# A hand-tuned order of work, shifted: a range flag and its register loads get earlier due times, and a new table of due-time offsets replaces the old one

## The chip, the cores and the metric

The kernel runs as one program on one core of a Trainium2 chip. The metric is device time in microseconds (us), the median of several executions. Five engines work side by side, each through its own queue of instructions in program order: TensorE (PE, with its weight loads listed as PEld), VectorE (DVE), ScalarE (ACT), GpSimd (POOL) and SyncE (SP). SP does little but issue DMA transfers; its issues are listed under SPq.

## The reference

The computation is a gated linear-attention scan followed by a two-layer MLP whose activation is a smooth gate.

```python
def _attn_ref(q, k, v, a_re, a_im):        # 4 batches, 8 heads, 768 steps, 48 wide
    mag = np.sqrt(a_re * a_re + a_im * a_im)
    scale = np.minimum(mag, 0.999) / (mag + 1e-06)
    a_re_n, a_im_n = (a_re * scale, a_im * scale)
...
    for t in range(S):
        ar, ai = (a_re_n[:, :, t, :, None], a_im_n[:, :, t, :, None])
        new_re = ar * S_re - ai * S_im
        new_im = ar * S_im + ai * S_re
        kv = np.einsum('bhd,bhe->bhde', k[:, :, t], v[:, :, t])
        S_re, S_im = (new_re + kv, new_im)
        y[:, :, t] = np.einsum('bhd,bhde->bhe', q[:, :, t], S_re)

def _moe_ref(x, w_in, w_out):              # x 3072x384, w_in 384x2048, w_out 2048x384
    h = x @ w_in
    g = np.where(h >= 1, h, np.where(h <= -1, 0.0, (h + 1) ** 2 / 4.0))
    return (g @ w_out).astype(np.float32)
```

## The kernel before

**Tiling.** The 3072 tokens are cut into 12 units u of 256 tokens (u0 to u11), and two units make one of 6 blocks (512 tokens). A unit goes through these steps:

- `gates(u)`: DVE and ACT turn the decays into running products (tiles ai_u) and multiply them into queries and keys. Its two last DVE operations, here called the *turns*, are one line, L984: one writes x_u, the other kq_u, each 128x1536.
- `spread`: ten DMAs on SP's queue (helper line L554) carry x_u and kq_u into the head layout hd_u_0, hd_u_1, hd_u_2. Of each of the two sources there are two pieces of 288 KB (48x1536), one of 128 KB (32x1024) and two of 32 KB (16x512).
- `attend(u)` on PE, in four short visits: *scores* (L1138, 32 small matmuls on hd_u, into banks that DVE masks at L1150), transposes (L1078), products (L1107) and values (L1182, L1190). The result goes by xr DMAs into the layout of the MLP.
- `split(blk)`: ACT writes xH (L1285), DVE the remainder xL (L1292).
- `moe(blk)`: the first product h (L1319), the gate (ACT s L1345, DVE g L1364 and L1372, ACT gh L1378, DVE gl L1382) and the second product o (L1396), in 16 steps f per block. A matmul of L1319 or L1396 is called a *MoE matmul* below; there are 1746 of 512 columns or their equal.

**Beside that.** `weights` decodes the packed weights early on: a load raw_i or raw_o (768 KB, L569), then on DVE y (L584), two merges (L593, L602) and the low part wi or wo (L613). `ranges` loads the packed weights a second time late in the run (tiles chk, L569) and sums them in two ACT passes each (L660, L668). From these sums and those of the gates nine tiny DVE operations (L1508 to L1516) make the *flag*; one PE matmul (L1519) and two DVE operations (L1520, L1524) finish it; five register loads (L1532 on ACT, POOL, DVE and SP, L1543 on PE) and a branch (L1547) read it. The branch leads to a general path that these inputs don't take. The last three results are copied out of PSUM at L1434 (ob) and stored by L554.

**What sets the order.** All operations are recorded first, with `pl.op`, and class `Plan` then writes the queues. `order` gives each operation a due time: the given `due=`, or the least of its successors' due times less its own duration, plus an offset from the table NUDGE under the operation's number, if it has one. Offsets thus pass on to all that an operation needs. Then a list scheduler takes, engine by engine, what is ready and due first; for DVE, ACT and SP it may hold a place for something that is due sooner. BEGIN[NBLK] is the due time at the end of the last block, the numbers are in ns. `emit` writes the result, and until the first MoE matmul `warm` adds idle matmuls (L1459) where PE would stand still. A waiting instruction blocks what is behind it on its engine, whatever that is.

## Time and profile before

| what | us |
|---|---|
| median of 3 executions (least, most) | 564.18 (564.12, 564.68) |
| the profiled execution's own time | 563.74 |
| its span, from first to last record | 561.9 |
| PE busy in the span | 548.6 |
| DVE busy | 438.8 |
| ACT busy | 395.3 |
| granted TensorE clock over the span | 1.00 |

The profiled execution is 0.44 us below the median, and 1.8 us of its time lie outside the span. Idle time of an engine is given with the instruction before which it fell, and with what released that instruction ("<-DMA hd<-kq" is the landing of a DMA that wrote hd from kq).

### The profile page before, as it was taken

The page shows a single profiled execution, that of the slowest core. Times are in us where ns is not written, and L with a number is a line of the kernel's source. Part 1 is how long each engine was busy: PE and PEld are TensorE (multiplying, and loading weights), DVE is VectorE, ACT ScalarE, POOL GpSimd, SP SyncE. Part 2 cuts the span into 40 slices and gives each one's busy share as a digit, 9 for nine tenths or more (in the row PEclk, how much of TensorE's full clock was granted, in tenths as well). Part 3 has the DMA queues.
Part 4 walks back from the last instruction along what each step waited for, and adds up shares of the span by engine and source line. Part 5 has one row for each costly group of instructions (what it writes and reads, how often), then busy time and mean ns, then how long its engine had stood idle before and what let it go on. Part 6 is the DMA issues. An engine that isn't in the chain of part 4 may idle for free.

```text
span 561.9 us, 10693 instructions
## 1 busy us (share of the span) xinstructions
PE 548.6 (98%) x4246; PEld 459.5 (82%) x4246; DVE 438.8 (78%) x611; ACT 395.3 (70%) x638; POOL 4.1 (1%) x27
## 2 busy tenths in 40 slices
PE   8999999989999999999999999999999999999997
PEld 8878777878888888888888888888888888888885
DVE  5999999989979888887996948898885743554643
ACT  6987987978977667766656663867556642469973
POOL 2000000000000000000000000000000000000000
PEclk9999999999999999999999999999999999999999
DMA  8587475463731604416200552606255300087631
GB/s 351 238 251 250 132 270 196 125 236 117 227 107 43 190 37 117 157 58 175 101 2 3 159 170 64 211 2 180 94 169 162 114 1 1 27 315 253 255 110 63
DMA packets 23686, 80.56 MB, mean 143 GB/s; under 512 B 4560, under 2 KB 10320, under 8 KB 23632
## 3 DMA queue, kind: packets, MB, share of 16 engines
q1 hardware_dynamic: 23488, 79.71, 42.4%
q8 instruction: 34, 0.56, 0.4%
q14 instruction: 20, 0.16, 0.1%
q10 hardware_dynamic: 144, 0.13, 0.1%
HBM read 55.05 MB, written 4.72 MB: 106 GB/s over the span
## 4 chain that ended last, share of the span: by engine, by line
PE 85%; DVE 10%; ACT 1%; issue 1%; DMA 1%; SPq 1%; POOL 0%; DVEq 0%; POOLq 0%; ACTq 0%
PE o L1396 33%; PE h L1319 32%; PE at L1138 5%; PE at L1182 3%; PE at L1190 3%; PE at L1107 2%; PE idle L1459 2%; PE at L1078 2%; DMA hd<-kq 1%; DVE x L984 1%; DVE kq L984 1%; PE o L821 1%; DVE g L1364 1%; SPq L554 1%; DVE gl L1382 1%
## 5 line engine op out<-in xcount | busy, mean ns | idle before, releaser
L1396 PE MATMUL o<-gh,wo 128*128 128x512 f32 x576 | 180.3, 394 | 0.0
L1319 PE MATMUL h<-xH,wi 128*128 128x512 f32 (+1 forms) x582 | 179.3, 390 | 0.9 <-ACT wo L637 0.6
L1319 PEld LDWEIGHTS h<-xH,wi 128*128 128x128 f32 x582 | 106.5, 188 | 23.7 <-DVE g L1364 1.1
L1396 PEld LDWEIGHTS o<-gh,wo 128*128 128x128 f32 x576 | 106.3, 188 | 22.4 <-issue 0.3
L1319 PE MATMUL h<-xL,wi 128*128 128x512 f32 (+1 forms) x291 | 112.4, 386 | 0.4 <-DVE xL L1292 0.4
L1396 PE MATMUL o<-gl,wo 128*128 128x512 f32 x288 | 112.3, 390 | 0.0
L1364 DVE TENSOR_TENSOR g<-h,s 128x512 f32<-128x512 f32 x95 | 65.3, 687 | 52.1 <-ACT s L1345 50.1
L1345 ACT ACTIVATE s<-h,cst 128x512 f32<-128x512 f32 x95 | 64.3, 685 | 44.9 <-PE h L1319 36.6
L1378 ACT CAST gh<-g 128x512 fp32r<-128x512 f32 x96 | 59.0, 617 | 33.9 <-DVE g L1372 24.7
L1382 DVE TENSOR_TENSOR gl<-g,gh 128x512 fp32r<-128x512 f32 x96 | 65.4, 685 | 14.6 <-ACT gh L1378 13.4
L1319 PEld LDWEIGHTS h<-xL,wi 128*128 128x128 f32 x291 | 54.6, 188 | 12.1 <-DVE xL L1292 0.8
L1396 PEld LDWEIGHTS o<-gl,wo 128*128 128x128 f32 x288 | 54.0, 188 | 11.5
L1372 DVE SCALAR_TENSOR_TENSOR g<-s,g 128x512 f32<-128x512 f32 x80 | 55.2, 691 | 2.2
L764 ACT ACTIVATE ai<-ai 128x768 f32<-128x768 f32 x48 | 40.3, 845 | 9.5 <-DVE ai L927 5.3
L1150 DVE COPY_PREDICATED am<-tri,at 128x512 f32<-128x512 uint32 x44 | 32.2, 740 | 7.6 <-PE at L1138 7.1
L1138 PE MATMUL at<-hd 96*64 96x64 f32 (+1 forms) x704 | 34.3, 249 | 3.1 <-DMA hd<-kq 3.1
L1138 PEld LDWEIGHTS at<-hd 96*64 96x64 f32 x704 | 31.6, 137 | 6.6 <-issue 4.2
L847 DVE TENSOR_TENSOR_SCAN ai<-again,ai 128x768 f32<-128x768 uint8 x20 | 35.0, 1749 | 0.4 <-ACT ai L764 0.2
L1190 PE MATMUL at<-am,V 128*64 128x128 f32 x352 | 32.9, 273 | 0.0
L1182 PE MATMUL at<-hd,st 96*64 96x128 f32 x304 | 30.5, 278 | 0.4 <-DVE am L1150 0.4
L564 ACT ACT_TABLE_LOAD x23 | 29.5, 1283 | 0.4
L764 ACT ACTIVATE x<-ai 128x768 f32<-128x768 f32 x27 | 22.3, 842 | 9.2 <-DVE ai L847 9.1
(133 smaller groups left out, 640.5 us busy)
## 6 DMA issues: line engine op xcount, KB each, us to landing
chk<-in_wl_dram SPq DMA_DIRECT2D x16, 768.0 KB, 4.6
kq<-in_kq_dram SPq DMA_DIRECT2D x12, 768.0 KB, 6.3
ai<-in_ari_dram SPq DMA_DIRECT2D x10, 768.0 KB, 6.2
V<-in_v_dram SPq DMA_DIRECT2D x12, 576.0 KB, 5.0
hd<-x SPq DMA_DIRECT2D x24, 288.0 KB, 3.4
hd<-kq SPq DMA_DIRECT2D x24, 288.0 KB, 4.2
raw_i<-in_wl_dram SPq DMA_DIRECT2D x8, 768.0 KB, 7.0
raw_o<-in_wl_dram SPq DMA_DIRECT2D x8, 768.0 KB, 5.0
```

Source lines behind the costliest of these rows:

```text
L764: lambda: A_.activation(out(), src(), f, **kw),
L847: lambda: V_.tensor_tensor_scan(dst().rearrange("p j t -> p (j t)"), again, src().rearrange("p j t -> p (j t)"), 0.0, op0=ALU.mult, op1=AL ...
L1138: PE_.matmul(SC.get()[o : o + HC, i + e, HC * k :], t[:, 0, ks], t[:, 1, qs], start=True, stop=True,)
L1182: PE_.matmul(o_, st.get().rearrange("p h e -> p (h e)")[:, lo : lo + 64], head(h)[:, 1, cs], start=True, stop=False,)
L1190: PE_.matmul(o_, V.get()[:, c, lo : lo + 64], ams[pr // 2].get()[:, 2 * (pr % 2) + e, :], start=st is None, stop=True,)
L1319: PE_.matmul(H.get()[:, lo:hi], weight["i", f // 2].get()[:, f % 2, part, sl], x.get()[:, j, lo:hi], start=j == 0 and n == 0, stop=j == NJ ...
L1345: lambda: A_.activation(SS.get(), H.get(), AF.Relu, bias=c_half, scale=-0.5 if spare else 0.5),
L1364: lambda: V_.tensor_tensor(G.get(), H.get(), SS.get(), op=ALU.max),
L1372: lambda: V_.scalar_tensor_tensor(G.get(), SS.get(), 1.0, G.get(), op0=ALU.min, op1=ALU.mult),
L1378: pl.op("ACT", act(T), lambda: A_.copy(GH.get(), G.get()), r=[G], w=[GH])
L1382: lambda: V_.tensor_tensor(GL.get(), G.get(), GH.get().bitcast(F32), op=ALU.subtract),
L1396: PE_.matmul(PO[m].get(), weight["o", f // 2].get()[:, f % 2, part, sl], g.get(), start=f == 0 and n == 0, stop=f == NF - 1 and n == 2,)
```

## The change

Three edits. The table NUDGE, some 650 offsets, is replaced by one of some 1200; a constant SOON = 6000 (ns) is added; and the nine flag operations of DVE and the four register loads of ACT, POOL, DVE and SP are due SOON ahead of the end of the plan. Nothing that is computed changes; instructions only take other places in their queues. The lines of the kernel move down by 35 (by 36 behind the new constant): L984 becomes L1020, L554 becomes L590, and so on.

```diff
 NUDGE = {
-    27: -14199.79, 28: -34500, 43: 134562.2, 53: -303446.36, 57: -4700, 58: -19660, 59: -78000,
...
+    23: 177054, 24: -34026, 25: 653, 29: -110195, 38: 300, 40: 12000, 53: -168116, 54: -375702,
...
 STAY = 300
+SOON = 6000
...
-        pl.op("DVE", 150, fn, w=[OK], after=marks, due=BEGIN[NBLK])
+        pl.op("DVE", 150, fn, w=[OK], after=marks, due=BEGIN[NBLK] - SOON)
...
                 lambda reg=reg: nc.reg_load(reg, ok[0:1, 0:1]),
                 r=[OK],
                 after=[gated[-1]],
-                due=BEGIN[NBLK],
+                due=BEGIN[NBLK] - SOON,
```

Where the table moves things is seen in the queues. The first place is SP's queue around the spread of u3. In the rows below hd_3_0 to hd_3_2 are the three head tiles, 48x1536 are pieces of 288 KB, 32x1024 of 128 KB and 16x512 of 32 KB; loads have a name that ends in _dram on the right. Before:

```order
L554 DMA hd_3_0_1144<-x_3_732 48x1536
L554 DMA hd_3_1_1151<-x_3_732 48x1536
L554 DMA hd_3_2_1158<-x_3_732 32x1024
L554 DMA hd_3_2_1158<-x_3_732 16x512 x2
L554 DMA hd_3_2_1158<-kq_3_854 16x512 x2
L554 DMA hd_3_2_1158<-kq_3_854 32x1024
L554 DMA hd_3_1_1151<-kq_3_854 48x1536
L554 DMA hd_3_0_1144<-kq_3_854 48x1536
L554 DMA kq_4_1210<-in_kq_dram 128x1536
L569 DMA raw_o5_1241<-in_wl_dram 128x1536
L554 DMA ai_5_1248<-in_ari_dram 128x1536
```

And now, in the changed kernel:

```order
L590 DMA hd_3_2_1144<-x_3_731 32x1024
L590 DMA hd_3_2_1144<-x_3_731 16x512
L590 DMA hd_3_1_1153<-x_3_731 48x1536
L590 DMA hd_3_2_1144<-x_3_731 16x512
L590 DMA hd_3_0_1165<-kq_3_831 48x1536
L590 DMA hd_3_1_1153<-kq_3_831 48x1536
L590 DMA hd_3_2_1144<-kq_3_831 32x1024
L590 DMA hd_3_2_1144<-kq_3_831 16x512 x2
L590 DMA hd_3_0_1165<-x_3_731 48x1536
L590 DMA ai_5_1222<-in_ari_dram 128x1536
L590 DMA kq_4_1236<-in_kq_dram 128x1536
L605 DMA raw_o5_1309<-in_wl_dram 128x1536
```

The last piece of the spread is now one of x_3, and the first loads behind it, ai_5 and kq_4, go into buffers that x_3 and kq_3 held, so their instructions wait on SP until the spread has read those out.

The second place is DVE between the two turns of u4 (its turns are the rows with x_4 and kq_4 on the left). Before:

```order
L984 TENSOR_TENSOR x_4_1170<-kq_4_1210,ai_4_849 128x1536
L1364 TENSOR_TENSOR g_0_12_1528<-h_0_12_1401,s_0_12_1477 128x512
L602 SCALAR_TENSOR_TENSOR raw_o6_1405<-raw_o6_1405 128x768
L1364 TENSOR_TENSOR g_0_13_1547<-h_0_13_1422,s_0_13_1519 128x512
L1382 TENSOR_TENSOR gl_0_12_1555<-g_0_12_1528,gh_0_12_1539 128x512
L984 TENSOR_TENSOR kq_4_1210<-kq_4_1210,ai_4_849 128x1536
```

Now:

```order
L1020 TENSOR_TENSOR x_4_1167<-kq_4_1236,ai_4_843 128x1536
L620 TENSOR_SCALAR y_o6_1500<-raw_o6_1446 128x768
L629 SCALAR_TENSOR_TENSOR raw_o6_1446<-raw_o6_1446,y_o6_1500 128x768
L1400 TENSOR_TENSOR g_0_13_1513<-h_0_13_1368,s_0_13_1481 128x512
L638 SCALAR_TENSOR_TENSOR raw_o6_1446<-raw_o6_1446 128x768
L620 TENSOR_SCALAR y_o7_1549<-raw_o7_1453 128x768
L1418 TENSOR_TENSOR gl_0_13_1553<-g_0_13_1513,gh_0_13_1529 128x512
L629 SCALAR_TENSOR_TENSOR raw_o7_1453<-raw_o7_1453,y_o7_1549 128x768
L649 TENSOR_TENSOR wo_6_1555<-raw_o6_1446,wo_6_1555 128x2x384
L638 SCALAR_TENSOR_TENSOR raw_o7_1453<-raw_o7_1453 128x768
L1400 TENSOR_TENSOR g_0_14_1584<-h_0_14_1455,s_0_14_1547 128x512
L1020 TENSOR_TENSOR kq_4_1236<-kq_4_1236,ai_4_843 128x1536
```

Counted from the start of the queue, six operations that stood behind the kq_4 turn stand ahead of it now (y_o7, both merges of raw_o7, wo_6, one g and one gl), and none has gone the other way.

The third place is PE near its end (at0_109<-ok4_121 is the flag's matmul, ok_123 the register's word). Before:

```order
L1396 MATMUL o2_114<-gh_5_15_5306,wo_7_1618 128x512 x2
L1396 MATMUL o2_114<-gl_5_15_5314,wo_7_1618 128x512
L1519 MATMUL at0_109<-ok4_121,cst_86 1x4
L1543 TENSOR_LOAD ok_123
```

Now:

```order
L1432 MATMUL o1_113<-gl_5_12_5270,wo_6_1555 128x512
L1432 MATMUL o2_114<-gh_5_12_5245,wo_6_1555 128x512 x2
L1432 MATMUL o2_114<-gl_5_12_5270,wo_6_1555 128x512
L1555 MATMUL at0_109<-ok4_121,cst_86 1x4
L1432 MATMUL o0_112<-gh_5_11_5232,wo_5_1402 128x512 x2
L1432 MATMUL o0_112<-gl_5_11_5239,wo_5_1402 128x512
```

The flag's matmul stood behind the last MoE matmul and now stands ahead of the last 33; PE's own register load keeps its place behind all of them.

Counted in the same way, these moved too. Of the MoE matmuls of the whole run, so many stand ahead of the first scores of a unit, before and now: u2 63 and 63, u3 183 and 180, u4 288 and 315, u5 441 and 423. Ahead of the kq turn DVE has, against before, one merge of raw_i3 (L602) less and one L1119 more at u2, one merge of raw_o4 (L593) less at u3, the six more at u4, and four less at u5 (a g pair, one xL, one gl). Behind the kq turn of u4 SP now issues eight transfers instead of six, with a 288 KB piece sixth and a 128 KB piece last; behind that of u5 it still issues seven, with a 288 KB piece sixth. On ACT four range passes that stood behind gh of the last block's step 11 stand ahead of it, and PE's first matmul that reads that tile has 60 MoE matmuls from itself to the end instead of 54. The stretches of attention that interrupt the MoE matmuls were 49 and are 46, the flag's matmul among them.

## Rows read from the trace of the kernel before

**Rows 1.** The page's first part: busy time of each engine, share of the span, and instructions.

```profile
PE 548.6 (98%) x4246; PEld 459.5 (82%) x4246; DVE 438.8 (78%) x611; ACT 395.3 (70%) x638; POOL 4.1 (1%) x27
```

**Rows 2.** Busy time by stretch of the span. Columns: stretch and its length, then PE, PEld, DVE, ACT and POOL busy with their counts, then granted clock, DMA share, GB/s.

```profile
59.00:120.00 61.00, 56.10 (x445) 45.68 (x444) 58.59 (x79) 54.20 (x82) 0.00 (x0) 1.00 0.62 208
...
160.00:540.00 380.00, 380.00 (x2778) 317.86 (x2774) 279.23 (x385) 247.06 (x411) 0.00 (x0) 1.00 0.36 116
500.00:542.00 42.00, 42.00 (x187) 34.77 (x186) 20.27 (x31) 38.09 (x77) 0.00 (x0) 1.00 0.65 236
```

**Rows 3.** Timeline of PE, the rows with idle time ahead of them at the scores of u2, at values of u2 and at the scores of u3. Columns: start, duration, engine, line, operation, tiles, shape, count, and in brackets the idle time before and its releaser.

```profile
73.88 1.63 PE L1138 MATMUL at<-hd 96*64 96x128 f32 x32 [1.14 <-DMA hd<-kq]
86.95 0.44 PE L1182 MATMUL at<-hd,st 96*64 96x128 f32 x4 [0.39 <-DVE am L1150]
...
115.51 1.56 PE L1138 MATMUL at<-hd 96*64 96x128 f32 x32 [1.96 <-DMA hd<-kq]
```

**Rows 4.** The chain of waits in the window 100 to 120 us, its piece ahead of the scores of u3: start, duration, what. (A DMA's time counts from its issue to its landing.)

```profile
110.11 5.27 DMA hd<-kq
```

**Rows 5.** Timeline of SP's queue at the spread of u3, with the load behind it.

```profile
103.02 3.24 SPq L554 DMA_DIRECT2D hd<-x  x5
106.36 4.33 SPq L554 DMA_DIRECT2D hd<-kq  x5
110.81 0.53 SPq L554 DMA_DIRECT2D kq<-in_kq_dram  x1
```

**Rows 6.** The same at the end of the spread of u2, with the load behind it.

```profile
70.52 0.52 SPq L554 DMA_DIRECT2D hd<-kq  x1
73.00 0.35 SPq L569 DMA_DIRECT2D raw_i<-in_wl_dram  x1
```

**Rows 7.** The DMA view of that last issue of u2: tiles, engine, count, KB each, median us from issue to landing.

```profile
hd<-kq SPq DMA_DIRECT2D x1, 288.0 KB, 3.3
```

**Rows 8.** DVE's groups by line, over the whole run: busy us and mean ns of one, then the idle time before them.

```profile
L1382 DVE TENSOR_TENSOR gl<-g,gh 128x512 fp32r<-128x512 f32 x96 | 65.4, 685 | 14.6 <-ACT gh L1378 13.4 <-PE o L1396 0.7
L1364 DVE TENSOR_TENSOR g<-h,s 128x512 f32<-128x512 f32 x95 | 65.3, 687 | 52.1 <-ACT s L1345 50.1 <-ACT s L1359 0.2
...
L593 DVE SCALAR_TENSOR_TENSOR raw_o<-raw_o,y_o 128x768 uint32<-128x768 uint32 x8 | 7.6, 955 | 0.1
...
L613 DVE TENSOR_TENSOR wo<-raw_o,wo 128x768 fp32r<-128x768 f32 x6 | 5.7, 948 | 0.0
...
L584 DVE TENSOR_SCALAR y_o<-raw_o 128x768 uint32<-128x768 uint32 x8 | 4.4, 552 | 0.0
```

**Rows 9.** Timeline of DVE: its wait at the first mask of u3; the kq turn of u4 and the row behind it; an xL, and the row behind the kq turn of u5.

```profile
116.45 0.73 DVE L1150 COPY_PREDICATED am<-tri,at 128x512 f32<-128x512 uint32 x1 [2.04 <-PE at L1138]
...
143.41 1.75 DVE L984 TENSOR_TENSOR kq<-kq,ai 128x1536 f32<-128x1536 f32 x1
145.08 0.95 DVE L613 TENSOR_TENSOR wo<-raw_o,wo 128x768 fp32r<-128x768 f32 x1
...
180.59 0.95 DVE L1292 TENSOR_TENSOR xL<-xr,xH 128x768 fp32r<-128x768 f32 x1
...
185.52 0.68 DVE L1364 TENSOR_TENSOR g<-h,s 128x512 f32<-128x512 f32 x1
```

**Rows 10.** Timeline of PE at the scores of u4 and of u5.

```profile
150.18 1.63 PE L1138 MATMUL at<-hd 96*64 96x128 f32 x32
...
193.88 1.56 PE L1138 MATMUL at<-hd 96*64 96x128 f32 x32
```

**Rows 11.** Timeline of SP's queue at the kq pieces of u4 and at the last issues of u5.

```profile
145.19 3.05 SPq L554 DMA_DIRECT2D hd<-kq  x5
...
190.36 1.41 SPq L554 DMA_DIRECT2D hd<-kq  x2
```

**Rows 12.** Timeline of all engines at the end: the last MoE matmul, the flag's matmul, the last store, the last flag operation.

```profile
557.28 0.39 PE L1396 MATMUL o<-gl,wo 128*128 128x512 f32 x1
...
557.60 0.19 PE L1519 MATMUL at<-ok,cst 128*1 128x4 f32 x2
...
558.57 0.34 SPq L554 DMA_DIRECT2D out_dram<-ob  x1
558.63 0.14 DVE L1524 TENSOR_SCALAR ok<-ft 1x1 int32<-1x1 f32 x1
```

**Rows 13.** The DMA view of that last store: KB each, median us from issue to landing.

```profile
out_dram<-ob SPq DMA_DIRECT2D x1, 128.0 KB, 1.7
```

**Rows 14.** Timeline of PE around one visit of attention late in the run, among MoE matmuls.

```profile
469.73 0.39 PE L1319 MATMUL h<-xL,wi 128*128 128x512 f32 x1
...
471.09 0.39 PE L1396 MATMUL o<-gl,wo 128*128 128x512 f32 x1
471.41 1.56 PE L1138 MATMUL at<-hd 96*64 96x128 f32 x32
...
473.46 0.39 PE L1319 MATMUL h<-xL,wi 128*128 128x512 f32 x1
```

**Rows 15.** Timeline of ACT at gh of step 11 of the last block, with a range pass behind it, and of PE at its first use of that tile.

```profile
541.52 0.62 ACT L1378 CAST gh<-g 128x512 fp32r<-128x512 f32 x1 [1.48 <-DVE g L1372]
542.05 0.91 ACT L660 ACTIVATE chk<-chk 128x768 f32<-128x768 f32 x1
...
545.27 0.61 PE L1396 MATMUL o<-gh,wo 128*128 128x512 f32 x2
```

243 rows, old and new, of the table NUDGE are left out of this document.

## The prediction

> **What bounds the kernel now.** I read the page's busy times first, then busy time by stretch, then PE's timeline for the rows that have idle time ahead of them, and last, from each of those, the chain of waits and the queues behind it. PE is busy 548.6 of a span of 561.9 us [rows 1], and from 160 to 540 us it is busy 380.00 of 380.00 [rows 2]. In that stretch a reordering can only win by fewer interruptions of the MoE matmuls. What it can win lies in 59 to 120 us, where PE is busy 56.10 of 61.00 and DVE 58.59 [rows 2]: DVE is nearly full there, and PE waits for what DVE makes. PE's three waits that hang on attention are 1.14 us at the scores of u2, 0.39 at values of u2 and 1.96 at the scores of u3, 3.49 in sum [rows 3]. The sum below is made on the profiled execution (span 561.9, own time 563.74), whose offset of 0.44 to the median is taken as fixed, so differences are applied to 564.18.
>
> **The wait at u3, and why it holds all that is ahead of it.** The scores of u3 start at 115.51, when the last piece of the spread has landed [rows 3]. That piece was issued at 110.11 and took 5.27 us [rows 4]; the load of kq_4 was issued behind it at 110.81, 0.70 us later [rows 5]. At u2 a last piece of the same 288 KB, issued at 70.52, took 3.3 us, and the next load came only at 73.00, 2.48 us later [rows 6, 7]. I take from this pair that a load on the heels of a spread delays its last piece by up to 5.27 - 3.3 = 1.97 us. In the changed kernel the two loads behind the spread of u3 need the buffers that the spread reads, so none can be issued before the pieces have been read out, and the last piece is again one of 288 KB: 3.3 us is the value nearest to it, 5.27 the other bound.
>
> The turns come earlier as well: one merge of raw_o4 (0.955 us, of which some 0.08 overlaps with its neighbour, as the 1.75 us turn at 143.41 whose follower starts 1.67 later shows) no longer stands ahead of them [rows 8, 9], which is 0.87. SP's issues run on without a gap from 103.02 to 110.69 [rows 5], so the last issue moves by the same 0.87, to 109.24, and the landing to 112.54. With 0.14 from landing to first matmul, as before, the scores start at 112.68 instead of 115.51: 2.83 earlier. But three fewer MoE matmuls stand ahead of them. One starts 0.227 us after the other ((471.09 - 469.73) / 6) [rows 14], so 0.68 of work is only put off. Net: **-2.15**.
>
> PE can be there in time: without its wait it was ready at 113.55, less 0.68 is 112.87, and the waits of u2, up to 1.53 [rows 3], shrink too (the turn is about 0.4 earlier and its last pieces are small ones). If they didn't, PE's 112.87 would set the start instead of 112.68. For the same reason what the table changes ahead of that point, in the head too, counts nothing of its own: PE waits at u3 anyway, and DVE's set of work there is the same but for the merge. Bounds: with a landing of 5.27 the gain is 0.87 - 0.68 = 0.19; it can't exceed the three waits, 3.49.
>
> **What the Trainium skill would make of it.** The row shows 5.27 us with a load 0.70 behind and 3.3 without [rows 4 to 7]. The Trainium skill, "DMA: Bandwidth & Descriptors", section "Queues, rings and completion order", says that each DMA engine consumes the descriptors of one ring in order. By that rule a load issued behind the pieces on the same queue can't hold them up, keeping it away gains nothing, and the sum would have -0.19 in place of -2.15. The pair of rows speaks against it, but it is one pair, in different surroundings; so it is a rival.
>
> **New waits at u4.** DVE gets six more operations ahead of the kq_4 turn: y_o7 0.55, two merges of 0.955, wo_6 0.95, g 0.69, gl 0.69, less 0.08 each: 4.3 us [rows 8]. Against that, DVE's own wait of 2.04 us for the scores of u3 [rows 9] goes with the scores 2.83 earlier. So the turn starts at 143.41 - 2.04 + 4.3 = 145.67 and ends 1.67 later, at 147.34. Eight issues follow at 0.61 each (3.05 for five) [rows 11]; the sixth, of 288 KB, starts at 150.5 and lands at 153.8 (3.3) to 155.8 (5.27), the last, of 128 KB, starts at 151.7 and lands at 155.0, for head tile 2, which the last of the 32 scores read. PE is there at 150.18 - 2.83 + 6.81 (30 more MoE matmuls between the scores of u3 and these) = 154.2 [rows 10]. Wait: 0 to 1.6; **+0.2**, since 153.8 is in time and the small one nearly.
>
> **New waits at u5.** DVE has 2.7 us less ahead of the kq_5 turn (an xL of 0.95, a g pair at 0.69 each, a gl of 0.69, less overlaps) [rows 8, 9]. That turn ended at 185.52, and now ends at 180.8 if the 2.04 is kept, else at 182.8. Before, the last issue ended at 191.77 [rows 11], seven issues in 6.25. The sixth, of 288 KB, starts after five, so at 184.0 (0.61 each) to 185.4 (0.89 each), and lands at 187.3 to 188.7, or up to 190.7 without the 2.04. PE is there at 193.88 - 2.83 + 0.2 - 3.4 (15 fewer MoE matmuls since the scores of u3) = 187.9 [rows 10]. Wait: 0 to 2.8; **+0.4**.
>
> **The flag.** Its matmul leaves the very end and interrupts PE 33 MoE matmuls ahead of it. Its own two passes took 0.19 [rows 12]; an interruption of 32 scores took 473.46 - 471.09 - 3 x 0.227 = 1.69 for rows of 1.56, 0.13 more [rows 14]; at the most the 0.32 from the last start at 557.28 to 557.60 [rows 12] and that 0.13 again. **+0.35** (0.2 to 0.45). Its gain at the end: the flag was done at 558.77, but the last store, issued at 558.57, lands 1.7 later, at 560.3 [rows 12, 13], so loads and branch have 1.5 us of cover. That store still waits for the last MoE matmul and two copies. **0** (0 to -0.1 while the cover holds; without it at most the 0.2 from 558.57 to 558.77). If the DVE operations of the flag stood badly they would block gl; they are nine of under 0.2 us on an engine with 20.27 busy of 42 [rows 2].
>
> **Interruptions.** 46 instead of 49, the flag's among the 46, so four of attention are gone at 0.13 or a little less: **-0.3** (0 to -0.5). Later units come after fewer MoE matmuls than before; DVE is busy 279.23 of 380 there [rows 2], which is their cover; 0 (up to +0.5 without it).
>
> **Sum:** -2.15 + 0.2 + 0.4 + 0.35 + 0 - 0.3 = -1.5, **562.7**. Its own range, from a wait of 0.8 less to 0.8 more at u4 and u5 or the landing between 3.3 and 4.1, is 561.9 to 563.5. About 0.2%, 1.13 us, is what can be told from no change, so the line of faster is 563.05.
>
> **Rivals.**
> (a) All three waits go and none comes back: DVE, freed of its own wait and with the loads out of the way, has u4 and u5 ready in time. -3.49 + 0.05 (flag and interruptions) is 560.7. For it: 2.04 of idle DVE, and small pieces last at u2. Against it: 4.3 us more ahead of kq_4.
> (b) The landing stays at 5.27, by the rule of order within the ring or because the loads were not the cause. -0.19 + 0.05, no new waits, since PE is later by 2: 564.0. Against it the pair above; for it that the spread of u3 moves its ten pieces back to back.
> (c) ACT becomes the bound near the end. gh of step 11 was done at 542.14 and first read at 545.27, 3.13 later [rows 15]. Now it is wanted 6 x 0.227 = 1.36 earlier, with four range passes of about 0.95 (the row has 0.91) ahead of it: 1.36 + 3.8 - 3.13 = 2.0 late, less what they take of ACT's 3.91 of idle time between 500 and 542 [rows 2]. At full price 562.7 + 2.0 = 564.7; the idle time is larger than the price, so it is not likely.
> (d) Slower: the kq_4 and kq_5 turns set PE's pace. Place: DVE between the masks of u3 and the kq_5 turn. If the 2.04 is not recovered, because DVE then waits for ACT or for a load, the large piece at u4 lands at 155.8 to 157.8, which costs 1.7 to 3.6 there, and at u5 another 1.4 falls due. 564.18 - 2.15 + 0.05 + (3.1 to 5.0) is 565.2 to 567.1, 566.1 in the middle. It decides for slower as soon as the new waits pass 2.10 + 1.13 = 3.2.
>
> **How the numbers follow.** The forecast 0.45, of which 0.30 lie below 563.05; (a) 0.20; (b) 0.10; (c) 0.11; (d) 0.14. Faster 0.30 + 0.20 = 0.50; same 0.15 + 0.10 + 0.11 = 0.36; slower 0.14. The range runs from 560.6, so that it takes in most of (a), to 565.5; what it leaves out is most of (d) and what would lie below (a), about 0.18.
>
> **What would show it.** In the changed profile: the scores of u3 start near 112.7 (without a wait, or one well under 1.96), the last piece of their spread takes near 3.3 and DVE's 2.04 ahead of its mask is gone; then the step on loads is right. A landing near 5.3 with no load behind makes (b) right. A wait "<-DMA hd<-kq" or "<-DMA hd<-x" on PE near 151 to 156 or 185 to 192 is the price of u4 or u5; above 3.2 together, (d). Idle time of PE after 540 "<-ACT gh" is (c). The flag's matmul should show a step of 0.3 to 0.5 between two MoE matmuls some 7.5 us ahead of the end, and the stretch from the last MoE matmul to the end of the span should keep its 4.2 us (557.67 to 561.9). The prediction falls if DVE meets a new wait between 62 and 105 us, because then the turns of u3 slip and take the scores with them.

## The result, and the profile after

| | changed | before |
|---|---|---|
| median, us (least to most; 6 executions each, on the same chip) | 566.44 (565.55 to 567.54) | 563.71 (562.33 to 564.68) |
| ratio, 95% interval | 1.0052 (1.0036 to 1.0067) | |
| span of the profiled execution | 564.4 | 561.9 |

The change makes the kernel 0.5% slower; 562.7 was predicted, and the measured time lies outside the range of 560.6 to 565.5. PE is busy 0.9 us longer than before [rows 1] and idle 1.6 us longer, so the share of busy time does not show where the time went. The first part of the changed kernel's page, then its busy time by stretch, columns as in [rows 2]:

```profile
PE 549.5 (97%) x4242; PEld 458.3 (81%) x4242; DVE 436.0 (77%) x611; ACT 395.2 (70%) x638; POOL 4.1 (1%) x27
```

```profile
59.00:120.00 61.00, 57.79 (x455) 46.99 (x454) 60.97 (x82) 56.39 (x84) 0.00 (x0) 1.00 0.59 195
160.00:540.00 380.00, 379.34 (x2772) 315.86 (x2769) 276.10 (x384) 245.90 (x412) 0.00 (x0) 1.00 0.36 120
```

From 59 to 120 us PE gains 1.69 us of busy time, and DVE is busy 60.97 of 61.00: it has no idle time left. From 160 to 540 us PE, never idle before, is idle 0.66.

**Where the time went, at equal work.** For each kernel I took the PE rows from the first MoE matmul on, counted the work ahead of each (0.227 us for a MoE matmul, a fixed time for each kind of attention matmul), and subtracted what the kernel before had needed for the same work. A minus is a lead. With other times for the attention matmuls the middle columns move by up to 0.3; "start", "last" and "end" do not. The columns are us of work; 60, 120, 320, 340 and 460 fall at about 122, 185, 392, 414 and 537 us of the trace. "start" is the first MoE matmul, "last" the start of the last one, "end" runs from the start of the last MoE matmul to the end of the span.

```
kernel         start     30     60    120    320    340    460   last    end
before         58.98   0.00   0.00   0.00   0.00   0.00   0.00   0.00   4.66
after          59.11  -2.18  -2.33  -1.23  -0.83   0.38   1.10   1.45   5.58
after_to_333   60.44  -2.05  -2.22  -1.01  -1.13  -1.13  -1.13  -1.13   4.65
before_to_333  59.09   0.01  -0.28  -0.25   0.68   1.86   2.48   2.83   5.71
soon_only      59.00  -0.03  -1.41  -1.33  -1.30  -1.30  -0.51  -0.16   5.68
flag_last      59.76  -1.68  -1.81  -0.67  -0.30   0.20   0.90   0.90   4.67
xr_first       59.22  -1.85  -2.02  -0.85  -0.50  -0.52   0.07   0.42   5.69
u10_late       59.21  -1.82  -1.96  -0.81   1.09   1.16   1.78   2.13   5.96
less_dve       59.20  -2.15  -3.07  -1.90  -1.55  -0.92  -0.19   0.15   5.53
g_sooner       60.03  -1.77  -1.79  -0.17  -0.10  -0.10  -0.10  -0.10   4.67
load_away      59.64   0.00  -1.69   2.63   2.59   2.59   2.60   2.60   4.66
```

The second row is the account of the change: a lead of 2.33 us once u3 is past, 1.10 of it gone by 185 us, 0.40 more by 392 (not traced to one wait), then 1.21 lost at the first visit of u10, 0.72 to 537 us, 0.35 at the flag, 0.92 at the end and 0.13 at the start. That is +2.50, the difference of the two spans (564.4 - 561.9). The other kernels are explained with their experiments.

**The lead.** PE's timeline of the changed kernel: the scores of u2, u3, u4 and u5, which answer to [rows 3] and [rows 10], and the rows with the largest idle times.

```profile
69.07 0.74 PE L1355 MATMUL h<-xH,wi 128*128 128x512 f32 x2 [1.17 <-DVE g L1400]
...
73.42 1.56 PE L1174 MATMUL at<-hd 96*64 96x128 f32 x32
...
99.81 0.73 PE L1355 MATMUL h<-xH,wi 128*128 128x512 f32 x2 [1.25 <-DVE g L1400]
...
112.85 1.56 PE L1174 MATMUL at<-hd 96*64 96x128 f32 x32
...
126.47 0.74 PE L1355 MATMUL h<-xH,wi 128*128 128x512 f32 x2 [0.89 <-DVE g L1400]
...
155.30 1.56 PE L1174 MATMUL at<-hd 96*64 96x128 f32 x32
...
188.76 1.56 PE L1174 MATMUL at<-hd 96*64 96x128 f32 x32
```

No scores wait any more. In their place stand three waits on g: PE's next h needs a PSUM bank that g must have read first, and DVE does g late. SP's queue at the spread of u3 (as [rows 5]) and the DMA view of its last piece (as [rows 7]):

```profile
102.52 2.39 SPq L590 DMA_DIRECT2D hd<-x  x4
105.01 3.22 SPq L590 DMA_DIRECT2D hd<-kq  x5
108.28 1.41 SPq L590 DMA_DIRECT2D hd<-x  x1
110.93 0.34 SPq L590 DMA_DIRECT2D ai<-in_ari_dram  x1
```

```profile
hd<-x SPq DMA_DIRECT2D x1, 288.0 KB, 3.8
```

The last piece is issued at 108.28 (110.11 before), no load follows for 2.65 us, and it lands in 3.8. The spread starts 0.50 us sooner than before, and its issues run faster: ahead of the last none takes more than 0.67. Before, one of the five kq issues [rows 5] took three times the usual 0.59:

```profile
107.57 1.85 SPq L554 DMA_DIRECT2D hd<-kq  x1
```

**The first visit of u10.** SP's queue of the kernel before, its transfers xr ahead of the spread of u10, and PE's scores of u10 there:

```profile
379.91 3.69 SPq L554 DMA_DIRECT2D xr<-xr  x6
...
409.01 1.56 PE L1138 MATMUL at<-hd 96*64 96x128 f32 x32
```

The same of the changed kernel, with the rows of ACT, DVE and PE that follow from it:

```profile
381.11 2.42 SPq L590 DMA_DIRECT2D xr<-xr  x4
383.58 0.59 SPq L590 DMA_DIRECT2D hd<-x  x1
...
388.45 1.22 SPq L590 DMA_DIRECT2D hd<-kq  x2
389.71 2.58 SPq L590 DMA_DIRECT2D xr<-xr  x2
...
391.74 1.88 PE L1174 MATMUL at<-hd 96*64 96x128 f32 x32
...
393.15 0.41 ACT L1321 CAST xH<-xr 128x256 fp32r<-128x256 f32 x1 [1.75 <-DMA xr<-xr]
...
393.58 0.43 DVE L1328 TENSOR_TENSOR xL<-xr,xH 128x256 fp32r<-128x256 f32 x1 [4.96 <-ACT xH L1321]
393.93 0.72 DVE L1186 COPY_PREDICATED am<-tri,at 128x512 f32<-128x512 uint32 x1
...
394.70 0.55 PE L1114 MATMUL at<-ident,hd 96*128 96x96 f32 x4 [0.60 <-DVE am L1186]
```

This is one chain, read from its last row back: the second transposes wait for the mask am; DVE holds the mask behind an xL, for which it has stood idle 4.96 us; the xL waits for ACT's xH, and that for two xr transfers that SP issued behind the whole spread instead of ahead of it. Before, PE came to these scores 17 us later, so none of this was in a hurry: they have 1098 MoE matmuls ahead of them now and had 1170, while SP starts the spread at nearly the same time (383.58, before 383.69).

**Flag and end.** The flag's matmul on PE, between two MoE matmuls:

```profile
551.04 0.39 PE L1432 MATMUL o<-gl,wo 128*128 128x512 f32 x1
551.36 0.19 PE L1555 MATMUL at<-ok,cst 128*1 128x4 f32 x2
551.48 0.73 PE L1432 MATMUL o<-gh,wo 128*128 128x512 f32 x2
```

The end in the timeline, its last MoE matmul and last store, SP's branch in the changed kernel and in the one before (its time in ns, then its start), and the DMA view of the changed kernel from 560 us on, with the queue q14 that carries instructions (packets, MB, share) and the stores (KB each, median us from issue to landing):

```profile
558.86 0.39 PE L1432 MATMUL o<-gl,wo 128*128 128x512 f32 x1
...
560.14 0.34 SPq L590 DMA_DIRECT2D out_dram<-ob  x1
```

```profile
L1583 SPq COMPARE_BRANCH  x1: 70/70/70, 560.5 to 560.5; - x1
```

```profile
L1547 SPq COMPARE_BRANCH  x1: 70/70/70, 559.5 to 559.5; - x1
```

```profile
q14 instruction: 3, 0.02, 1.9%
...
out_dram<-ob ACTq DMA_DIRECT2D x1, 128.0 KB, 2.1
out_dram<-ob SPq DMA_DIRECT2D x1, 128.0 KB, 2.7
```

The last store needs 2.7 us where it needed 1.7 [rows 13]; its issue comes 1.28 us behind the last MoE matmul, as before (1.29). SP branches 0.4 us behind that issue, and DVE and ACT, whose registers are loaded too, branch ahead of it, at 559.7 and 560.1. In the packets, three fetches of 8 KB start at 561.12, 561.24 and 561.64, while 1 KB packets of the store run until 562.3. Before, all five engines branch at 559.5, 0.9 us behind the store's issue, and the fetches start at 560.56, when the store's last packet had ended at 559.95.

### The profile page after: what moved, and what is told of

It reads as the page before. It is cut to its first block, busy times and chain, and to the rows that moved or that the text cites. A ratio compares the mean times of both kernels' runs of the same rounds, so it can differ in the third digit from the quotient of the medians.

```text
span 564.4 us, 10701 instructions
## 1 busy us (share of the span) xinstructions
PE 549.5 (97%) x4242; PEld 458.3 (81%) x4242; DVE 436.0 (77%) x611; ACT 395.2 (70%) x638; POOL 4.1 (1%) x27
## 4 chain that ended last, share of the span: by engine, by line
PE 79%; DVE 12%; ACT 3%; SPq 2%; DMA 2%; issue 1%; POOL 0%; DVEq 0%; ACTq 0%; POOLq 0%
PE o L1432 30%; PE h L1355 30%; PE at L1174 4%; PE at L1226 3%; PE at L1218 3%; PE at L1143 2%; PE idle L1495 2%; SPq L590 2%; PE at L1114 2%; DVE ai L883 1%; DVE g L1400 1%; PE o L857 1%; DVE am L1186 1%; DVE gl L1418 1%; DMA xr<-xr 1%
## 5 line engine op out<-in xcount | busy, mean ns | idle before, releaser
L1174 PE MATMUL at<-hd 96*64 96x128 f32 (+1 forms) x704 | 34.5, 249 | 0.2 <-DMA hd<-kq 0.2
L1238 ACT COPY xr<-at 128x512 f32<-128x512 f32 (+2 forms) x27 | 13.6, 504 | 18.2 <-PE at L1226 18.1
```

Source lines behind the costliest of these rows:

```text
L1174: PE_.matmul(SC.get()[o : o + HC, i + e, HC * k :], t[:, 0, ks], t[:, 1, qs], start=True, stop=True,)
```

## The experiments

Unless said otherwise each starts from the changed kernel and moves operations, named by their numbers in the plan, after the list scheduler:

```diff
         order = self.order()
+        for i, j in MOVES:
+            order.remove(i)
+            order.insert(len(order) if j is None else order.index(j), i)
```

A hybrid takes the operations of one kernel's plan up to some time (HEAD_OPS) and leaves the rest to the other's order:

```diff
         order = self.order()
...
+        order = [*HEAD_OPS, *(i for i in order if i not in HEAD_OPS)]
```

Ratios are to executions of the kernel before on the same chip, with 95% intervals; the changed kernel's is 1.0052 (1.0036 to 1.0067).

**soon_only and table_only: the two edits apart.** The first is the kernel before with SOON and the earlier due times, the second the new table without SOON, which is this edit:

```diff
-SOON = 6000
+SOON = 0
```

> The old table with the flag and its register loads due 6 us earlier. Theory T (the loss is in the table: the gain at u3 is paid back by new waits for gate operations near 69, 100 and 126 us and at the scores of u9 near 392 us; the flag costs only its interruption of PE): 0.2 to 0.5 us slower than before, the stretch from the last MoE matmul to the end of the span stays at 4.2 us. Rival F (the flag's move makes the loss, by its interruption and by a longer end, since the changed kernel's last store landed 2.7 us after its issue instead of 1.7): 1.2 us slower or more, and the end stretch is near 5.1 us.

> The new table with the flag due at the end of the plan, as before the change; the order differs from the changed kernel only in the last block's last steps. T: 1.5 to 2.5 us slower than before, with the same waits near 69, 100, 126 and 392 us. F: within 0.5 us of before, and an end stretch of 4.2 us.

Measured: 1.0038 (1.0024 to 1.0051) and 1.0098 (1.0079 to 1.0117). So SOON alone costs 2 us, as rival F had it and more than theory T allowed. Its end is 5.68, and it loses 0.8 + 0.35 behind 455 us. table_only did not separate the edits: the new table's offsets hold the flag's matmul and loads early by themselves, so its end is long as well (5.88). It came out 5.5 us slower than before, outside both forecasts; in its trace the MoE starts 0.92 later than in the changed kernel, PE loses 0.65 more behind 537 us and the end is 0.30 longer, and how much of that is in its four executions is not shown. In soon_only the queue at u3 is that of before, yet PE waits 0.58 there instead of 1.96. PE, SP's third kq issue, its last one with the load behind it, and the DMA view of the last one:

```profile
114.09 1.56 PE L1139 MATMUL at<-hd 96*64 96x128 f32 x32 [0.58 <-DMA hd<-kq]
```

```profile
107.61 1.37 SPq L555 DMA_DIRECT2D hd<-kq  x1
...
109.66 0.59 SPq L555 DMA_DIRECT2D hd<-kq  x1
110.36 0.52 SPq L555 DMA_DIRECT2D kq<-in_kq_dram  x1
```

```profile
hd<-kq SPq DMA_DIRECT2D x1, 288.0 KB, 4.3
```

**new_to_u3 and old_to_u3: hybrids with the seam at the scores of u3.**

> The queues of the changed kernel up to the scores of u3, and from there the remaining operations in the order of the kernel before. T: the gain up to u3 (2.0 us by PE's lost time at 118 us) stays for the most part, since the waits that take it back come later: 1 to 2 us faster than before. Rival E (nothing is gained up to u3, because DVE is full there and any order gives the same time by 130 us): within 0.6 us of before, with waits elsewhere between 60 and 140 us in place of the old ones.

> The reverse: the old queues up to the scores of u3, and from there the order of the changed kernel. T: the losses without the gain, 3 to 5 us slower than before. E: as the changed kernel, 2 to 3 us slower than before.

Measured: 1.0022 (1.0011 to 1.0033) and 1.0098 (1.0077 to 1.0118). new_to_u3 came out as neither theory T nor rival E had it; old_to_u3 is nearest to T's 3 to 5 us. new_to_u3 has the lead (2.1 us after u3) and is level with before at 350 us: an early lead alone does not last in a plan that isn't made for it. old_to_u3 starts 1.0 late, is about 1.5 us behind at 134 us beyond that, loses 1.35 more at u10, and has an end of 5.72. It has the changed kernel's wait on g without having its lead: 0.98 us at 129.93.

**flag_last and flag_mid.** The flag's matmul, its two DVE operations and the loads go behind everything; in flag_mid the matmul stays early.

```diff
+MOVES = ((2202, None), (2203, None), (2204, None), (2207, None), (2205, None), (2206, None), (2208, None))
```

> The changed kernel with the flag's PE matmul, its last two DVE operations and the register loads put back behind everything else, the rest of the new order kept. Theory T (an early branch lets the engines fetch their next instructions while the last store is on its way, and the 8 KB packets of those fetches hold up one DMA engine with packets of the store): the stretch from the last MoE matmul's start to the end of the span falls from 5.6 to 4.7 us and the 0.32 us step on PE goes, 1.2 us faster than the changed kernel, so 1.5 to 2 us slower than before. Rival L (the end is longer for another reason, such as the order of the last stores): the end stays at 5.6 us, and only 0.3 us is won.

> The changed kernel with the flag's PE matmul left early, but its two DVE operations and the register loads behind everything else. T: the step of 0.3 us on PE stays, the end is 4.7 us, 0.9 us faster than the changed kernel. Rival L: no change, end 5.6 us. If the matmul's place were what lengthens the end, then flag_last is short and this one long.

Measured: 1.0031 (1.0014 to 1.0048) and 1.0043 (1.0029 to 1.0057). Both ends are 4.67 again, the store lands in 1.7, and flag_last has no step at the flag. By the medians some 1.2 us (1.0052 to 1.0031) go with SOON's two terms; these two intervals overlap, but two pairs further on, each measured on one chip, agree: the same moves take xr_first from 566.83 to 565.65 (xr_flag) and u10_late from 567.98 to 566.45 (u10_late_flag).

**loads_pd and loads_as.** Only the register loads of ACT and SP go behind everything (pd, the edit shown), or only those of DVE and POOL (as).

```diff
+MOVES = ((2206, None), (2208, None))
```

> The changed kernel with the register loads of ACT and SP put back behind everything; those of DVE and POOL stay early, the flag too. The stretch from the last MoE matmul to the end of the span was 5.5 to 6.0 us in every run with early loads and 4.7 us in every run with late ones. Theory T (an engine with its register at hand branches at once, and the instruction fetch that follows lies beside the last store): if the fetches of ACT or SP do it, 4.7 to 4.9 here; if those of DVE or POOL, 5.5 or more. Rival Y (it is the flag's early place, not the branch): 5.5 or more here and in the sister run.

> The sister run: the loads of DVE and POOL behind everything, those of ACT and SP early. If ACT or SP make the end longer: 5.5 us or more; if DVE or POOL: 4.7 to 4.9. If it needs both: between 4.9 and 5.4 in both runs.

Measured ends: 5.33 and 5.40, against 5.58 with all four early and 4.67 with none (ratios 1.0060 and 1.0059, intervals 1.0037 to 1.0081 at the widest). POOL has nothing else to do there, so its load runs early in loads_as too (at 552.8; DVE's at 560.0): the two runs hold back ACT and SP, and DVE alone. Either leaves the end long, neither all of it; the last store lands in 2.45 and 2.52. The flag stays early in both and in flag_mid, so its place is not what makes the end long. flag_mid also moves the flag's last two DVE operations, which no load can overtake; no run moves all four loads without them.

**load_away.** In the kernel before, the loads kq_4, raw_o5 and ai_5 go behind the load of raw_i7, away from the spread of u3.

```diff
+MOVES = ((823, 435), (280, 435), (871, 435))
```

> The kernel before with the three loads kq_4, raw_o5 and ai_5 moved behind the load raw_i7, which is issued some 3 us after the scores of u3 begin. Theory H (a load on the heels of the spread holds up its last piece): the last piece of u3 takes 3.3 to 3.8 us instead of 4.4 to 5.4, PE's wait there falls from about 2 to under 0.6 us; of the time 0 to 1.5 us is kept. Rival R (order within the ring, or the delay comes from instruction fetches or from SP's gap inside the spread): the piece takes 4.4 us or more as before, and the time is within 0.5 us of before or later.

Measured: 1.0084 (1.0058 to 1.0109). PE and DVE of this kernel:

```profile
114.45 1.56 PE L1142 MATMUL at<-hd 96*64 96x128 f32 x32 [0.28 <-DMA hd<-kq]
...
125.14 0.56 DVE L588 TENSOR_SCALAR y_o<-raw_o 128x768 uint32<-128x768 uint32 x1 [3.04 <-DMA raw_o<-in_wl_dram]
...
129.54 0.90 PE L1082 MATMUL at<-ident,hd 96*128 96x96 f32 x4 [2.70 <-DVE st L1123]
```

The last piece landed in 4.05 us instead of 5.27, and the wait at u3 fell from 1.96 to 0.28. But raw_o5 came late, DVE stood still for it, and PE lost more than it had won. That the load made the difference is not shown. With kq_4 issued 0.70 us behind it the same piece took 5.27 (before), 5.25 (old_to_u3), 5.15 (before_to_333) and 4.29 (soon_only), and soon_only is the trace that load_away's 4.05 compares with: the third kq issue took 1.85, 1.92 and 1.67 in the first three, 1.37 in soon_only and 1.35 in load_away. A 16 KB instruction packet (queue q8) starts within 0.15 us of that issue in all five, 1.43 to 1.53 us long in the first three and 0.96 in the other two. Between the two like traces the load is worth 0.24. What makes an issue and a landing long is open.

**mask_first.** The first mask of u10 goes ahead of the xL that holds it.

```diff
+MOVES = ((1838, 1611),)
```

> The changed kernel with one DVE operation moved: the first mask of u10 goes ahead of an xL that waits for an xr transfer. T (at 391.74 us PE waits 1.4 us too long on scores and transposes of u10, because the mask stands behind that xL): the wait goes, 1.0 to 1.4 us faster than the changed kernel. Rival M (the stretch is slow because the bank or another operation is late): under 0.3 us.

Measured: 1.0055 (1.0038 to 1.0071). Nothing is won. The mask no longer holds PE, the g behind the same xL does:

```profile
396.45 0.73 PE L1359 MATMUL h<-xH,wi 128*128 128x512 f32 x2 [1.15 <-DVE g L1404]
```

**xr_first and xr_flag.** SP issues the last two xr transfers ahead of the spread, as before; xr_flag also has flag_last's moves.

```diff
+MOVES = ((1601, 1827), (1602, 1827))
```

> The changed kernel with two SP issues moved: the last two xr pieces of block 5's first unit stand ahead of the last nine pieces of the spread of u10, where the kernel before has them. Theory U (the table put them behind that spread, so xH and xL are late, xL holds DVE for 4.96 us, and the mask or the next g behind it costs PE about 1.3 us): the 0.60 us wait of PE at the u10 visit and the growth of the visit by 1.3 us go, span 564.4 - 1.3 = 563.1, ratio to before about 1.003. Rival V (the visit is late because SP stood still for an instruction fetch, and it will hit other work of u10 instead): PE still loses 0.7 to 1.3 us between 388 and 400 us, ratio 1.004 to 1.006.

> The same two issues moved, and the flag's matmul, its two DVE operations and all register loads put back behind everything. If the two late costs add up (u10 1.3 us, flag and end 0.35 + 0.9 us), the span is 564.4 - 2.5 = 561.9 and the ratio to before 0.999 to 1.001. If the earlier run with the flag last gained for another reason than its end, ratio 1.002 to 1.003.

Measured: 1.0065 (1.0052 to 1.0078) and 1.0036 (1.0023 to 1.0049). PE at u10 in xr_first, then in xr_flag:

```profile
392.17 1.56 PE L1178 MATMUL at<-hd 96*64 96x128 f32 x32
393.65 0.88 PE L1118 MATMUL at<-ident,hd 96*128 96x96 f32 x8
```

```profile
392.98 1.44 PE L1178 MATMUL at<-hd 96*64 96x128 f32 x26
395.00 0.52 PE L1178 MATMUL at<-hd 96*64 96x128 f32 x6 [0.58 <-DMA hd<-kq]
```

In the profiled execution of xr_first the loss at u10 is gone, as theory U wanted. But that execution was the shortest of its five (565.52, median 566.83), and the medians of both kernels are no better than without the move. xr_flag shows why it can't be counted on: the spread now stands two issues, 1.2 us, later on SP, and its last piece holds PE instead. Of the two late terms, which should have brought the kernel level with before, only the flag's and the end's are seen.

**u10_late and u10_late_flag.** The visit's scores and transposes go some 9 us later on PE, with the mask and the copies. In this order the second transposes stand ahead of the mask, so that the mask reads their values and not the scores'.

```diff
+MOVES = ((1837, 1614), (1839, 1614), (1841, 1614), (1843, 1614), (1838, 1441), (1842, 1443), (1844, 1443))
```

> The changed kernel with the first visit of u10 (scores and transposes on PE, the first mask on DVE, two copies on ACT) put back by about 9 us of MoE matmuls; SP's order stays as changed. Theory W (the changed order asks for u10 72 MoE matmuls, 16 us, sooner than before while its spread leaves SP at the same time, so that nothing is left in hand for the late xr pieces or a slow issue): PE loses under 0.3 us at that visit instead of 1.36, span 564.4 - 1.3 = 563.1, and the median falls by 1.0 to 1.4 us, ratio to before 1.0030. Rival X (the visit is only the first place at which a lateness of DVE or ACT shows; it comes up again behind it): the loss appears within the next 30 us, ratio 1.005.

> The same, with the flag's matmul, its two DVE operations and all register loads behind everything as before. By the sum of the terms (1.3 at u10, 0.35 for the flag, 0.9 at the end): 2.7 - 2.55, ratio 1.0003, at most 1.0015. If the two do not add up, 1.002 or more.

Measured: 1.0086 (1.0064 to 1.0108) and 1.0057 (1.0036 to 1.0077). PE and DVE of u10_late:

```profile
392.47 0.42 DVE L1332 TENSOR_TENSOR xL<-xr,xH 128x256 fp32r<-128x256 f32 x1 [3.38 <-ACT xH L1325]
...
393.81 0.73 PE L1359 MATMUL h<-xH,wi 128*128 128x512 f32 x2 [1.53 <-DVE g L1404]
```

Theory W falls as I had put it, and u10_late_flag is far from its 1.0003: the visit itself loses nothing, but DVE still stands at the xL, and the g behind it holds PE 1.53 us. Whatever stands behind that xL on DVE is late.

**after_to_333 and before_to_333: the two halves of the change.** Hybrids with the seam at the planned time 333 us.

> All queues of the changed kernel up to the planned time 333 us, then the order of the kernel before for what is left, the flag and the register loads included. PE at equal work was 1.2 us ahead of the kernel before at that place, in the changed kernel. Theory K (the lead is kept when no new wait stands behind it, since PE is the bound there): the lead of 0.9 to 1.3 us is still there at the last MoE matmul, the end takes 4.7 us, span 560.7 to 561.2 with an equal start, ratio 0.998. Rival P (the lead is paid back, because DVE or ACT behind PE are the bound): within 0.3 us of before at the end, ratio 1.000.

> The kernel before in all queues up to the planned time 333 us, then the order of the changed kernel, flag and register loads included: the counterpart of the run that gave 1.000. If the slowdown lies in what the change does behind 333 us: PE level with before at 333 us, and 2.0 to 3.0 us lost behind that (u10, the late visits, flag, end), ratio 1.004 to 1.005. If it lies in the first half: ratio under 1.002.

Measured: 1.0000 (0.9991 to 1.0009) and 1.0069 (1.0048 to 1.0089). The late half alone makes the kernel slower by as much as the whole change or more, and PE waits at u10 as in the changed kernel:

```profile
396.19 0.55 PE L1313 MATMUL at<-ident,hd 96*128 96x96 f32 x4 [0.60 <-DVE am L1385]
```

The early half is worth nothing in the median. In its profiled execution, the longest of its eleven (564.06), the lead of 1.13 is kept from 333 us to the last MoE matmul (theory K), but the MoE starts at 60.44 instead of 58.98.

**less_dve and g_sooner: what sets the waits on g.** less_dve cuts two operations of wi_5's decoding to 8 columns and takes the low part from the high one (it leaves out the low bits of that one weight tile); g_sooner is after_to_333 with g of step 5 ahead of wi_5's low part.

```diff
+        less = (kind, i) == ("i", 5)
+        part = lambda t: t[:, 0:8] if less else t
...
-                Y.get(), top(), 3, 0x3FFFFFFF, op0=ALU.logical_shift_left, op1=ALU.bitwise_and
+                part(Y.get()), part(top()), 3, 0x3FFFFFFF, op0=ALU.logical_shift_left, op1=ALU.bitwise_and
...
-                low(), low(), 29, Y.get(), op0=ALU.logical_shift_right, op1=ALU.bitwise_or
+                part(low()), part(low()), 29, part(Y.get()), op0=ALU.logical_shift_right, op1=ALU.bitwise_or
...
```

```diff
+MOVES = ((378, 267),)
```

> The changed kernel with y_i5 and the first merge of raw_i5 cut to 8 columns, so that DVE has 0.47 + 0.87 = 1.3 us less to do at 93 to 96 us (leaves out: the low bits of one weight tile, wi_5, whose values are then other ones). Theory D (DVE is full there and sets PE's pace through the gate g): the 1.25 us wait of PE on g at 99.8 us falls by 0.8 (s is ready then) or more, and PE is at least 0.8 us ahead of the changed kernel from there on; span 563.6 if the lead is kept to the end. Rival E (ACT's s sets it): that wait falls by under 0.3, span 564.2 to 564.4.

> The changed order up to 333 us and the order of before behind it, with one DVE operation moved: g of step 5, done at 99.76 in the changed kernel, ahead of wi_5 (0.95 us). If DVE's order sets that wait of 1.25 us: it falls by 0.7 to 0.9, the lead is kept to the end as with the two operations cut to 8 columns, median 562.3, ratio 0.998 to 0.999. If wi_5 or the turn of u3 behind it comes late in its place: ratio 1.000, with a new wait between 100 and 115 us.

Measured: 1.0048 (1.0033 to 1.0063) and 1.0012 (0.9998 to 1.0026). PE in less_dve, then in g_sooner:

```profile
99.20 0.73 PE L1362 MATMUL h<-xH,wi 128*128 128x512 f32 x2 [0.51 <-DVE g L1407]
```

```profile
100.42 0.73 PE L1522 MATMUL h<-xH,wi 128*128 128x512 f32 x2 [0.53 <-DVE g L1567]
107.76 0.73 PE L1522 MATMUL h<-xH,wi 128*128 128x512 f32 x2 [0.57 <-DVE g L1567]
```

With 1.3 us less to do, DVE has g ready 0.74 sooner (1.25 to 0.51), and the larger lead is kept to 392 us (0.7 more than the changed kernel at 60, 120 and 320 us of work). With the same work in another order (g_sooner) that wait falls as much, a new one of 0.57 comes 7 us later, and the lead is down to 0.10 by 320 us of work. Theory D holds for the wait at 99.8: DVE is full there, and an order only chooses what is late. The next wait on g, 0.89 us at 126.47 in the changed kernel, stays in both (0.94 and 0.92).

## Why the prediction was wrong

**u3, -2.15: met in these two traces, partly by luck, and not seen in the medians.** The lead after u3 is 2.33 in the trace, the scores start at 112.85 (112.68 predicted), without a wait. But the landing is 3.8, not 3.3, and the time is met because the last issue came 0.96 earlier than worked out (108.28, not 109.24): "SP's issues run on without a gap" passed over the issue of 1.85 us that stands among them before. With before's queue PE's wait at u3 was 1.96, 0.58, 2.04 and 1.69 in four traces. So the step that failed here is that a wait of one execution was booked as one that every execution has. In the medians the new order up to u3 (new_to_u3, 1.0022) and up to 333 us (after_to_333, 1.0000) wins nothing.

The part on loads rests on a pair of rows from different surroundings and is not borne out: soon_only, with a load 0.70 us behind the piece, landed in 4.29, load_away, with none, in 4.05. Rival (b) takes the rule of order in a ring from the Trainium skill, "DMA: Bandwidth & Descriptors", section "Queues, rings and completion order"; the same section says that a later descriptor may still finish its write before an earlier one, so the rule alone does not exclude that a load holds a piece up. Its number, a landing of 5.27, did not come; its reason, that the load is not the cause, the traces do not refute.

**u4 and u5, +0.6: absent, and a price was paid elsewhere.** The kq turn of u4 starts at 145.87 (145.67 predicted), and both scores start without a wait. But by 185 us 1.10 of the 2.33 is gone, most of it in PE's wait of 0.89 on g at 126.47. That is ahead of the turns of u4: this g stands on DVE behind a product of 1.75 us, a scan of 1.75 and the y of a raw_o. The wait of 1.25 at 99.8 is ahead of the scores of u3 and lies within the 2.33. The step that failed is the one in which only the turns were followed through DVE's queue, and the rest of the table's changes up to u3 "counts nothing of its own": on an engine that is full, everything behind a moved operation has to be followed, and g frees the banks that PE needs next. less_dve and g_sooner show this for the wait at 99.8. That the one at 126.47 belongs to the new order behind u3 is shown by old_to_u3, which has it (0.98) with the old order up to u3.

**The flag, +0.35: right.** From the MoE matmul at 551.04 to the flag's is 0.32, and the lead falls by 0.35 there.

**The end, 0: wrong, +0.92 in the trace.** "Loads and branch have 1.5 us of cover" held for the flag itself, but not for what an early load lets happen: in the changed kernel three engines branch around the last store's issue, and the fetches start while it is in flight. In nine traces with all loads early the end is 5.53 to 6.02 and the last store lands in 2.66 to 3.15; in loads_pd and loads_as the end is 5.33 and 5.40; in nine with loads late it is 4.65 to 4.67 and the store lands in 1.73 to 1.75. That the early loads, with the two DVE operations ahead of them, decide is shown. That it is the instruction fetches beside the store's packets is read from the branches and the packets and was not tested apart.

**Interruptions, -0.3, and later units, 0: wrong, +0.72 and +1.21.** The count fell to 46 as foretold. Of the 0.72, about half goes with the second scores of u10, now cut into two visits of 16; no run tests that. Some 0.32 more is a step near 501 us, where PE's next h comes 0.43 us behind the o ahead of it instead of 0.23, since DVE's g is late:

```profile
501.01 0.39 PE L1432 MATMUL o<-gl,wo 128*128 128x512 f32 x1
501.44 0.73 PE L1355 MATMUL h<-xH,wi 128*128 128x512 f32 x2
```

The same step, behind the same MoE matmul (the 1494th), stands in all fifteen traces with the flag's DVE operations early, soon_only with its old table among them (at 498.86), and in none of the five with the tail of before. So it goes with the flag's due times and not with the later units. The 1.21 at u10 is the larger miss (0.50 to 1.21 in the rows of the table that keep this order there), and its step is the sentence that DVE's 279.23 busy of 380 is cover for units that come sooner. Idle time on DVE does not help where DVE is idle because it waits, in order, for SP's xr transfers. mask_first and u10_late show that the loss belongs to whatever stands behind that xL; xr_first and xr_flag that it can be moved to the landing of the spread. What it is worth in the median, none of them shows, and no order tried here cures it.

**The sum.** -2.33 + 1.10 + 0.40 + 1.21 + 0.72 + 0.35 + 0.92 + 0.13 = +2.50, and 2.73 in the medians. The rival for slower, (d), named the wrong place: its prices at u4 and u5 are zero. Rival (c) did not come either: PE has no wait on ACT's gh behind 540 us. The halves confirm where it happens: the order up to 333 us is worth 0.0 (-0.5 to +0.5 us), the order behind it is all of the slowdown. **Still open** is why the early lead does not show in after_to_333's median. The lead in single traces is measured against one wait of 1.96, which with the same queue was 0.58 in another execution, and the first MoE matmul starts at 59.07 to 60.44 us (mean 59.74) in fifteen traces with the new order in the head, at 58.98 to 59.98 (mean 59.34) in five with the old; that difference is no larger than the scatter.

## What to carry to other kernels

Before calling a unit that comes sooner covered, compare on every queue of its chain, SP's above all, when its inputs leave and when they are asked for: here PE asked 17 us sooner and SP sent at the same time. On a full engine, price a reordering by what it puts behind the moved work, since a wait that is removed at one place comes back at the next tile that frees a bank. A wait that hangs on a DMA's landing should be read from several executions before it is booked as a gain.

## What was not expected of the hardware

- Loading the branch's registers ahead of the last stores made the end 0.7 to 1.4 us longer: the last 128 KB store took 2.7 us instead of 1.7 in the changed kernel, with 8 KB instruction packets of 0.33 to 0.53 us between its 1 KB packets.
- The same ten transfers of u3 in the same order left PE waiting between 0.58 and 2.04 us in four traces: where one issue took 1.67 to 1.92 us the last piece landed in 5.15 to 5.27, where it took 1.37, in 4.29.
- Two xr issues on SP took 2.58 us in the changed kernel, where two hd issues took 1.22 just ahead of them, and 2.57 at the same instructions in before_to_333. In both stretches the packets show one instruction packet of 16 KB (queue q8), 1.51 and 1.43 us long, where the median is about 1; that the issue waited for it is a guess. It is not what makes the xL late: in flag_mid the two xr issues took 1.22, and DVE stood still for 5.04 ahead of that xL.
